# Batch 1's pairs 0 and 1 transposed by DMA instead of TensorE, with a third buffer for transposed keys and a new order of steps

## The chip, the cores and the metric

The kernel runs on one core of a Trainium2 chip. A core has five engines with an instruction queue each: TensorE (PE) multiplies matrices, VectorE (DVE), ScalarE (ACT) and GpSimd (POOL) work on elements, and SyncE (SP) only issues DMAs. GpSimd issues DMAs as well. The metric is the device time of one execution in microseconds (us); less is better.

## The reference

Attention with a sliding window of 96 keys and 8 global keys (4 batches, 8 heads, 768 tokens, head width 64), with a linear bias by distance, and behind it a SwiGLU block (512 to 1536 to 512) on all 3072 tokens. Inputs and outputs are 32-bit floats.

```python
scores = scale * np.matmul(q, k.transpose(0, 1, 3, 2))
rel = pos[:, None] - pos[None, :]
is_global = pos[None, :] < int(n_global)
is_local = (rel >= 0) & (rel < int(n_local))
dist = np.where(is_global & ~is_local, float(n_local), np.abs(rel).astype(np.float32))
scores = scores + (-slopes[:, None, None] * dist[None, :, :])[None, :, :, :]
scores = np.where(is_global | is_local, scores, -1000000000.0)
a = softmax(scores)            # with max subtracted
x = np.matmul(a, v), heads side by side: 3072 x 512
g = x @ w_gate
out = (g * sigmoid(g) * (x @ w_val)) @ w_out
```

## The kernel before

**Layout.** Scores are computed transposed: keys on the partitions, queries along the free dimension. So q and k must stand in SBUF with the head width on the partitions, which is a transpose of what lies in DRAM. Two heads make a pair (0 to 3) and fill 128 partitions together. Keys are cut into 7 chunks of 120, each with the 8 global keys in front (`kT`, a tile for each pair, used again by every batch). Values lie by the same chunks in `vS`, a buffer for a batch, three buffers in turn. Tokens of the SwiGLU block go in 8 stages of 384 (two for a batch).

**One list sets the order.** The whole program is a list of 1,092 named steps, the string `ORDER` (from line 37), read from left to right at the end of the kernel; the dictionary `WORK` maps a step's name to a function. A step `name.a.b` calls the function with these arguments. No scheduler moves anything: each engine executes its instructions in the order in which the list issues them, and waits at an instruction until its inputs and buffers are ready. The steps that matter here:

- Loads on GpSimd's queue (they convert from 32 to 16 bits on the way): `Lh` halves of heads of batch 0, `LG` all global values, `Lv.b.c` the values of batch b and chunk c (line 267), `L4.i.h` four heads of batch 1 at once (i is 0 for k, 1 for q), `Lr.b.i.h` the rows of one head (line 308), `Lw.w.n.g` parts of w_gate (w = 0) and w_val (w = 1) (line 315), `Lo.g` parts of w_out. `Lf`, `Li` and `Ld` are the first loads and the constants, on the queues of SyncE and ScalarE.
- Other work on GpSimd: `cast` where its last letter is P, `Z.b.P` (clears the tail of a value buffer) and `G.b.c0.c1.P` (copies global values into `vS`, line 282). A last letter V means VectorE, A ScalarE.
- `cast.i.p` converts first loads to 16 bits (line 352), `sl` and `M` make slopes and masks, `fill.n` runs n matmuls on constants.
- Batch 0 is transposed by TensorE: `T.p.half.i`, six transposes each, evacuated by `k` and `q`.
- Batch 1's pairs 0 and 1 are transposed by TensorE too: `U.p.i` (line 407, twelve transposes into one PSUM bank), evacuated by `kw.p` (keys) and `qw.p` (queries).
- All others go by DMA: `D.b.p.i` (line 435, on SyncE's queue) transposes pair p of the stage buffer. Queries go straight into `qT` (four buffers); keys go into `kN` (two buffers), from where `K.b.p` spreads them into the chunks of `kT` with three copies on VectorE (lines 442 to 446).
- Attention: `B` bias of batch 0 and `c.b.p.u` scores (TensorE, line 479), `x` exponentials (ScalarE), `m` masks (VectorE), `w.b.g.half.what` weighing (TensorE, line 540; what = 0 gives the sums, 1 and 2 the values), `n`, `i`, `r`, `p` divide by the sums and give `xT`.
- SwiGLU: `g.t.f` and `v.t.f` are the gate and value products of stage t and block f (four matmuls, line 590; `ga` and `gb` are halves of a `g`), `t` the tanh (ScalarE), `s` the sigmoid's product (VectorE, line 600), `h` the hidden row (VectorE), `o.t.i.part` the output product (three matmuls, line 631), `e` copies to SBUF and stores (SyncE's queue).

**Stage buffers.** A batch's k and q stand in `kst` and `qst` until they are transposed. These have two buffers each, dealt out in the order of the list: batch 0's first loads (32 bits) hold one and its other loads (16 bits) the second; batch 1 gets the first one again. Of batches 2 and 3, the one whose load comes first in the list gets the second one, and the other follows batch 1 in the first: its first load must wait until all K transposes of batch 1 have read there, and while it waits GpSimd's queue issues nothing behind it. Before, `Lr.2.0.0` is the earlier one and `Lr.3.0.1` the load that waits.

**The place of the change.** In the list before, the four `U` stand among the products of stage 1; `Lv.1.0` to `Lv.1.3` stand ahead of `Lr.3.0.1`, the load that waits for batch 1's stage buffer.

Of the kernel before, what the change touches and what calls it, by code (L numbers as in the profile page):

```python
# [42 lines left out]
c.0.3.0 x.0.2.0 T.1.1.0 Z.2.V Lh.1.1.4.8 T.1.1.1 c.0.2.1 x.0.3.0 G.0.1.4.V i.0.0.0 q.1.1.V T.0.1.1
B.3.1 c.0.3.1 T.0.1.0 Lv.0.3 k.1.1.A q.0.1.V k.0.1.V Lv.0.1 Lh.0.1.4.8 x.0.2.1 r.0.0.0 Lw.0.0.0
T.3.1.1 T.2.1.1 x.0.3.1 q.3.1.A c.0.1.3 c.0.0.2 w.0.1.0.0 i.0.1.0 Lw.0.0.1 q.2.1.A w.0.0.0.1
Lw.1.0.1 x.0.0.2 w.0.0.0.2 Lw.1.0.0 c.0.0.3 Lw.0.1.1 T.3.1.0 Lw.0.1.0 p.0.0.0.1.V r.0.1.0 T.2.1.0
Lw.1.1.0 x.0.1.3 x.0.0.3 Z.0.P p.0.0.0.0.V w.0.1.0.1 p.0.1.0.0.V w.0.1.0.2 p.0.1.0.1.V k.3.1.A
Lw.1.1.1 c.0.1.2 k.2.1.A ga.0.2 Lv.0.6 ga.0.0 ga.0.1 c.0.2.2 x.0.1.2 gb.0.0 m.0.0.2.V M.7.1 gb.0.1
# [12 lines left out]
x.1.1.1 h.1.1 o.0.0.0 v.1.11 g.1.9 v.1.9 s.1.5 v.1.5 g.1.7 t.1.7 g.1.3 t.1.9 Lr.1.1.6 m.1.0.1.V
D.1.2.1 m.1.0.0.V h.1.5 Lv.1.3 D.1.3.0 o.0.1.0 g.1.11 o.0.0.1 Lv.1.2 o.0.1.1 t.1.3 o.0.0.2 s.1.7
Lr.3.0.1 Lr.2.0.5 v.1.0 m.1.1.1.V o.0.1.2 o.0.1.3 D.1.3.1 t.1.11 s.1.9 s.1.3 s.1.11 o.0.0.3 h.1.0
v.1.3 h.1.11 m.1.1.0.V w.1.0.0.0 h.1.9 Lv.2.2 Lr.2.1.0 K.1.2 i.1.0.0 e.0.1 w.1.0.0.1 Lr.2.0.4 e.0.0
w.1.0.0.2 c.1.2.1 h.1.3 c.1.2.0 r.1.0.0 n.1.0.0 o.0.2.0 Lr.2.1.4 D.2.0.0 K.1.3 x.1.2.1 p.1.0.0.0.V
x.1.2.0 o.0.2.1 Lv.1.5 o.1.0.0 c.1.3.0 c.1.3.1 m.1.2.1.V c.1.0.2 o.0.2.2 o.1.0.1 x.1.3.0 m.1.3.0.V
# [38 lines left out]
o.4.1.1 s.5.8 o.4.1.2 h.5.6 v.5.8 x.3.0.2 o.4.1.3 t.5.9 p.3.1.0.0.V v.5.4 s.5.9 s.5.4 e.4.1 h.5.8
e.4.2 g.6.3 c.3.3.2 c.3.2.2 g.6.9 h.5.4 o.4.0.0 x.3.2.2 t.6.9 v.5.9 x.3.3.2 v.6.9 g.6.5 g.6.6 t.6.3
s.6.9 g.6.2 m.3.0.2.V h.6.9 g.6.1 t.6.6 t.6.5 s.6.6 g.6.4 o.4.0.1 o.4.0.2 v.6.5 s.6.3 m.3.3.2.V
s.6.5 t.6.1 v.6.4 t.6.2 h.5.9 v.6.1 g.6.8 o.4.0.3 s.6.1 h.6.5 s.6.2 m.3.2.2.V h.6.1 t.6.4 w.3.1.1.1
# [596 lines left out]
```

## Time and profile before

| | us |
|---|---|
| median of three runs | 240.96 |
| lowest and highest | 238.77, 241.08 |
| the profiled execution's own time | 239.84 |
| its span in the trace | 238.0 |

The span runs from the first to the last instruction that the profile has; some 1.8 us of the execution lie around it. The prediction shows lines of these views: the busy time of each engine (first the sum and the share of the span, then the number of instructions), strips of the span in 40 slices of 5.95 us with the busy share of each in tenths, the chain of waits that ended last, groups of instructions, and DMAs with their time from issue to landing. Rows of the chain and the timeline give the start, the length or busy time, the engine, the line of the code and the number of instructions; square brackets hold the idle time ahead of an instruction and what ended it. PE is TensorE, PEld its loading of weights, SPq the DMA queue of SyncE. The granted clock of TensorE was full in this execution (mean 1.0).

### The profile page before, as it was taken

What the parts mean: (1) busy time and instruction counts of PE and PEld (TensorE: products, weight loads), DVE (VectorE), ACT (ScalarE), POOL (GpSimd) and SP (SyncE); (2) the same over time, 40 slices, a digit from 0 to 9 for tenths busy, and PEclk for the clock granted to TensorE, in tenths of its full rate; (3) what the DMA queues carried; (4) which work ended last, traced back from release to release, by engine and by line L of the source; (5) the groups of instructions that cost most, each with busy time, mean ns of one, the idle gap of its engine ahead of it and who ended that gap; (6) DMA issues with size and microseconds to landing.
All of it is one profiled execution on the core that took longest, in us unless ns stands there. A gap on an engine that the chain in (4) does not pass through costs nothing.

```text
span 238.0 us, 5798 instructions
## 1 busy us (share of the span) xinstructions
PE 231.6 (97%) x2356; PEld 133.7 (56%) x2356; DVE 171.7 (72%) x411; ACT 117.5 (49%) x218; POOL 78.2 (33%) x99
## 2 busy tenths in 40 slices
PE   6999999999999999999999999999999999999994
PEld 4566566554556555555655654665555655555452
DVE  3799999767799976877948879889548854755400
ACT  3799813943776336377543366632453414223111
POOL 8874896720799845776000000000000000000000
PEclk9999999999999999999999999999999999999999
DMA  7999999999999999999974060100020101100114
GB/s 167 177 185 206 192 194 177 183 183 135 182 145 155 151 148 148 168 167 128 134 113 104 30 86 17 74 3 0 3 88 0 47 4 48 41 0 27 64 45 176
DMA packets 88715, 25.56 MB, mean 107 GB/s; under 512 B 78536, under 2 KB 85744, under 8 KB 88688
## 3 DMA queue, kind: packets, MB, share of 16 engines
q0 software_dynamic: 67520, 13.81, 70.9%
q1 hardware_dynamic: 20480, 10.80, 24.1%
q10 hardware_dynamic: 688, 0.59, 0.7%
q8 instruction: 18, 0.29, 0.6%
q14 instruction: 9, 0.07, 0.1%
HBM read 28.58 MB, written 6.29 MB: 146 GB/s over the span
## 4 chain that ended last, share of the span: by engine, by line
PE 89%; DMA 4%; ACT 3%; DVE 1%; issue 0%; SPq 0%; DVEq 0%; ACTq 0%
PE banks L590 52%; PE banks L631 25%; PE banks L540 5%; PE banks L479 4%; ACT at L489 2%; DMA dist<-dist_c 2%; DMA kN<-kst 2%; PE banks L620 1%; PE banks L466 1%; PE banks L369 1%; PE banks L407 1%; DVE xT L573 0%; DVE rb L563 0%; ACT masks L340 0%; ACT qT L398 0%
## 5 line engine op out<-in xcount | busy, mean ns | idle before, releaser
L596 ACT ACTIVATE th<-banks 128x384 f32<-128x384 f32 x96 | 44.7, 493 | 71.1 <-PE banks L590 68.0
L590 PE MATMUL banks<-xT,wv 128*128 128x384 f16 x384 | 72.7, 326 | 0.1
L590 PE MATMUL banks<-xT,wg 128*128 128x384 f16 x384 | 72.3, 326 | 0.1
L631 PE MATMUL banks<-wo,hT 128*128 128x512 f16 x276 | 68.0, 379 | 0.3 <-DVE sl L600 0.3
L606 DVE TENSOR_TENSOR hT<-banks,sl 128x384 f16<-128x384 f32 x96 | 51.5, 552 | 20.9 <-PE banks L590 19.5
L600 DVE SCALAR_TENSOR_TENSOR sl<-th,banks 128x384 f32<-128x384 f32 x96 | 50.3, 546 | 16.5 <-ACT th L596 15.7
L590 PEld LDWEIGHTS <-wv 128*128 128x128 f16 x384 | 37.1, 98 | 27.8 <-issue 0.7
L590 PEld LDWEIGHTS <-wg 128*128 128x128 f16 x384 | 36.8, 98 | 26.3 <-issue 0.3
L489 ACT ACTIVATE at<-banks 128x864 f16<-128x864 f32 (+2 forms) x52 | 42.1, 842 | 9.2 <-PE banks L479 8.6
L631 PEld LDWEIGHTS <-hT 128*128 128x128 f16 x276 | 26.1, 98 | 27.5 <-issue 1.5
L508 DVE TENSOR_TENSOR at<-at,masks 128x864 f16<-128x864 f16 (+3 forms) x60 | 25.5, 470 | 3.9 <-ACT at L489 3.7
L267 POOL DMA_DIRECT2D vS<-in_v_dram x28 | 25.4, 914 | 7.0 <-DMA vS<-in_v_dram 2.3
L649 ACT ACTIVATE osb<-banks 128x512 f32<-128x512 f32 x23 | 13.5, 598 | 25.0 <-PE banks L631 23.4
L308 POOL DMA_DIRECT2D kst<-in_k_dram x20 | 17.1, 855 | 16.7 <-PE banks L540 12.1
L308 POOL DMA_DIRECT2D qst<-in_q_dram x20 | 17.0, 858 | 3.6 <-DMA wo<-in_moe_w_out_dram 1.0
L479 PE MATMUL banks<-qT,kT 64*128 64x216 f16 (+5 forms) x240 | 14.4, 240 | 0.0
L573 DVE TENSOR_TENSOR xT<-ns,rb 128x384 f16<-128x384 f32 x24 | 12.6, 548 | 0.1
L479 PEld LDWEIGHTS <-kT 64*128 64x128 f16 x240 | 8.3, 94 | 7.4 <-issue 5.9
L540 PE MATMUL banks<-at,vS 128*32 128x216 f16 (+6 forms) x576 | 12.0, 225 | 0.4 <-issue 0.4
L549 ACT COPY ns<-banks 128x768 f32<-128x768 f32 x12 | 9.6, 799 | 4.8 <-PE banks L540 4.7
L540 PEld LDWEIGHTS <-vS 128*32 128x32 f16 x576 | 9.8, 95 | 2.6 <-issue 2.2
L556 DVE STREAM_TRANSPOSE dT<-banks 128x384 f32<-128x384 f32 x16 | 9.2, 575 | 1.4 <-PE banks L540 1.2
(59 smaller groups left out, 116.5 us busy)
## 6 DMA issues: line engine op xcount, KB each, us to landing
out_dram<-osb SPq DMA_DIRECT2D x23, 256.0 KB, 2.2
vS<-in_v_dram POOLq DMA_DIRECT2D x24, 120.0 KB, 7.6
qst<-in_q_dram POOLq DMA_DIRECT2D x20, 96.0 KB, 8.1
kst<-in_k_dram POOLq DMA_DIRECT2D x20, 96.0 KB, 7.4
wg<-in_moe_w_gate_dram POOLq DMA_DIRECT2D x6, 256.0 KB, 9.2
wv<-in_moe_w_val_dram POOLq DMA_DIRECT2D x6, 256.0 KB, 8.9
wo<-in_moe_w_out_dram POOLq DMA_DIRECT2D x3, 512.0 KB, 8.6
q<-in_q_dram POOLq DMA_DIRECT2D x3, 192.0 KB, 7.0
```

What stands on the lines that cost most here:

```text
L267: nc.gpsimd.dma_start(out=v_of(b)[NG:NG + n, c, :, :], in_=v[b, :, KC * c:KC * c + n, :].rearrange("h p d -> p h d"))
L308: nc.gpsimd.dma_start(out=rows_of(i, b, h // 2)[:, :, h % 2, :], in_=KQ[i][b, h].rearrange("(t p) d -> p t d", p=128))
L479: nc.tensor.matmul(sc[:, hi, col:col + n], lhsT=kTs[hp][r, 128 * c:128 * c + 128], rhs=qTs[b, hp][r, q0:q0 + n], start=fresh, stop=True, s ...
L489: nc.scalar.activation(out=at[:, :, 0:w], in_=scs.pop((b, hp, u))[:, :, 0:w], func=AF.Exp, scale=scale)
L508: ENG[e].tensor_mul(a2, a2, m[:, :, m0:m0 + n])
L540: nc.tensor.matmul(dst[r, o:o + n], lhsT=vSs[b][:, c, 4 * g + j, what - 1::2] if what else ones[:, 0:32], rhs=ats[b, hp, u][:, j % 2, col: ...
L590: nc.tensor.matmul(gv[t, f, which][:, 0:TB], lhsT=w[:, c, 128 * f:128 * f + 128], rhs=xTs[t][:, c, :], start=(c == 0), stop=(c == NC - 1))
L596: nc.scalar.activation(out=th, in_=gv[t, f, 0][:, 0:TB], func=AF.Tanh, scale=0.5)
L600: nc.vector.scalar_tensor_tensor(out=sl, in0=gv[t, f, "t"], scalar=1.0, in1=gv[t, f, 0][:, 0:TB], op0=AluOp.add, op1=AluOp.mult)
L606: nc.vector.tensor_mul(hTs[t][:, f, :], gv[t, f, 1][:, 0:TB], gv[t, f, "s"])
L631: nc.tensor.matmul(ops_t[t, i], lhsT=hTs[t][:, f, 128 * i:128 * i + 128], rhs=wo[:, f, :], start=(f == 0), stop=(f == NFF - 1))
L649: nc.scalar.mul(out=osb, in_=ops, mul=0.5)
```

## The change

- The steps `U`, `kw`, `qw` and `L4` leave the list; their functions stay in the code, unused.
- Batch 1's keys and queries of heads 0 to 3 are now loaded row by row (eight more `Lr.1`, so sixteen in all), and `D.1.0.0`, `D.1.0.1`, `D.1.1.0`, `D.1.1.1` transpose them by DMA, `K.1.0` and `K.1.1` spread the keys.
- `kN` has three buffers.
- The list is a new one from the first step on. In its head, the first loads and casts stand in another order and `cast.1.0` is on GpSimd instead of VectorE; `fill.14` and `fill.2` stand together; `G.0.4.7.P` stands among the weight loads instead of behind them. `Lr.3.0.4` stands ahead of all loads of batch 2, so that batch 3 gets the second `kst` buffer and batch 2 follows batch 1 in the first. `Lr.2.0.1`, the first load that needs batch 1's `kst` buffer again, stands ahead of `Lv.1.0` to `Lv.1.3`. Later parts are in another order too, with the same steps.
- The program has 2308 matmuls and transposes on TensorE in place of 2356, 24 DMA transposes in place of 20, and 98 loads on GpSimd's queue in place of 92.

The diff, cut to what is spoken of (a line of three dots stands for lines left out; the rest of the list holds the same steps as before in another order):

```diff
 ORDER = """
-Lf.A.1.1 Lf.S.0.1 LG pre cast.1.1.V fill.14 Li T.1.0.1 Lf.A.1.0 sl.3 cast.0.1.A sl.2 T.1.0.0 Ld.S
-B.1.0 Lf.S.0.0 B.1.1 k.1.0.V Lh.1.0.4.8 sl.1 cast.1.0.V fill.2 q.1.0.V cast.0.0.A sl.0 sl.6 sl.5
-T.0.0.1 c.0.1.1 T.0.0.0 c.0.1.0 M.3.1 T.3.0.1 T.2.0.1 q.0.0.A x.0.1.1 B.0.0 Lh.0.0.4.8 k.0.0.V B.0.1
...
-g.0.4 g.0.6 m.0.2.3.V Lw.1.2.0 g.0.5 h.0.1 v.0.6 G.0.4.7.P t.0.4 h.0.3 t.0.7 L4.0.0 M.3.0 s.0.4
-Lr.1.1.7 m.0.3.2.V v.0.5 v.0.7 r.0.0.1 v.0.4 g.0.9 t.0.6 t.0.5 s.0.7 s.0.5 s.0.6 L4.1.0 h.0.5 Z.3.P
-g.0.10 h.0.6 h.0.7 w.0.1.1.0 Lr.1.1.4 w.0.0.1.1 w.0.1.1.1 w.0.1.1.2 w.0.0.1.2 t.0.9 s.0.9 i.0.1.1
-Lr.1.0.6 p.0.0.1.0.V r.0.1.1 t.0.10 Lr.1.0.4 Lr.2.0.0 Lr.1.0.7 Lo.0 Lv.1.0 g.0.8 p.0.0.1.1.V
-Lr.2.0.1 g.0.11 v.0.10 p.0.1.1.1.V Lv.1.1 v.0.11 p.0.1.1.0.V t.0.11 g.1.8 s.0.11 h.0.11 t.0.8 g.1.1
-t.1.1 g.1.2 s.0.10 v.1.8 g.1.4 h.0.4 h.0.10 s.0.8 s.1.1 U.0.0 U.1.1 t.1.8 U.0.1 U.1.0 t.1.2 s.1.8
-Lo.1 qw.0.A s.1.2 Lr.1.0.5 Lr.1.1.5 g.1.6 M.4.0 h.1.8 v.0.9 kw.0.V qw.1.V M.6.0 M.7.0 v.1.2 g.1.0
-kw.1.A h.0.9 h.1.2 t.1.4 v.1.6 M.0.0 t.1.6 c.1.0.1 t.1.0 s.1.4 s.1.6 c.1.1.0 x.1.1.0 D.1.2.0 Z.1.V
...
+Lf.A.1.0 Lf.S.0.1 Li LG pre Lh.1.0.4.8 Lh.0.0.4.8 Lf.A.1.1 cast.1.1.V Ld.S Z.0.P cast.1.0.P sl.3
+fill.14 fill.2 sl.2 T.0.0.1 cast.0.1.A M.5.1 Lh.0.1.0.4 Lv.0.3 T.1.0.0 Lf.S.0.0 T.1.0.1 sl.0
+Lh.1.1.0.4 M.0.1 B.1.0 k.1.0.V cast.0.0.A sl.4 T.0.0.0 q.1.0.A B.1.1 M.3.1 c.0.1.1 q.0.0.A sl.1
...
+g.0.7 Lw.1.2.1 h.0.1 g.0.4 v.0.6 t.0.7 h.0.3 s.0.6 x.0.2.3 Lw.1.2.0 g.0.5 h.0.2 s.0.7 m.0.3.2.V
+v.0.5 t.0.4 Lo.0 m.0.3.3.V v.0.7 g.0.11 s.0.4 Lr.1.1.3 h.0.6 Lr.1.0.0 g.0.9 m.0.2.3.V w.0.1.1.0
+t.0.5 t.0.9 Lr.1.0.4 M.2.0 w.0.1.1.1 Lr.1.1.2 s.0.5 Lr.1.1.5 w.0.1.1.2 h.0.7 h.0.5 w.0.0.1.2
+Lr.1.0.6 w.0.0.1.1 g.0.8 i.0.1.1 Lr.1.0.5 v.0.10 p.0.0.1.0.V p.0.0.1.1.V t.0.11 v.0.4 t.0.8 s.0.11
+Lr.1.1.1 v.0.8 r.0.1.1 v.0.11 Lr.3.0.4 s.0.8 g.0.10 Lo.1 M.1.0 p.0.1.1.1.V t.0.10 Lr.1.0.3
+p.0.1.1.0.V g.1.8 s.0.9 M.0.0 v.1.8 t.1.8 g.1.3 h.0.8 h.0.4 Lr.1.1.4 t.1.3 s.1.8 g.1.9 Lr.1.1.0
+g.1.0 t.1.0 Lr.1.0.2 Z.1.V h.0.11 g.1.1 v.0.9 s.1.3 v.1.6 s.0.10 D.1.1.0 g.1.4 D.1.1.1 s.1.0 h.0.9
...
+g.1.7 D.1.2.0 s.1.1 v.1.9 g.1.6 h.1.1 Lr.1.0.1 Lo.2 h.1.4 g.1.11 t.1.7 h.1.9 g.1.2 s.1.7 o.0.0.0
...
+v.1.0 D.1.2.1 v.1.7 Lr.1.1.7 Lr.1.1.6 o.0.1.1 D.1.3.0 K.1.1 h.1.6 h.1.11 K.1.2 o.0.1.2 c.1.1.0
+D.1.0.0 c.1.1.1 Lr.2.0.1 Lv.1.2 M.7.0 h.1.0 Z.2.V Lv.1.0 o.0.1.3 Lv.1.1 K.1.3 x.1.1.0 x.1.1.1
+o.0.0.2 Lv.1.3 K.1.0 m.1.1.0.V o.0.0.3 c.1.2.0 Lr.2.1.0 D.1.3.1 D.1.0.1 e.0.1 Lr.2.0.4 c.1.2.1
...
+m.1.0.1.V o.1.0.2 w.1.0.0.0 Lr.3.1.4 Lr.2.0.5 w.1.1.0.2 r.1.1.0 w.1.1.0.1 w.1.0.0.1 w.1.0.0.2
...
@@ tr_dma
-            dst = kNs[b, hp] = sb2.tile([128, S], FP16, name="kN", tag="kN", bufs=2)
+            dst = kNs[b, hp] = sb2.tile([128, S], FP16, name="kN", tag="kN", bufs=3)
```

More of the change, by code (lines that the diff above doesn't have):

```diff
@@ L43 @@
[L43 to L48, printed above, removed]
@@ L61 @@
[L61 to L66, printed above, removed]
@@ L105 @@
[L105 to L108, printed above, removed]
-w.3.0.1.1 s.6.4 h.6.4 t.6.8 w.3.1.1.2 w.3.1.1.0 w.3.0.1.0 e.4.0 i.3.1.1 i.3.0.1 w.3.0.1.2 g.6.0
-n.3.1.1 v.6.0 v.5.2 v.6.6 r.3.1.1 t.6.0 n.3.0.1 g.6.10 r.3.0.1 h.5.2 p.3.0.1.1.V s.6.0 g.6.7 v.6.3
@@ new lines @@
+T.2.0.1 sl.5 k.0.0.V x.0.1.1 c.0.1.0 B.0.1 c.0.0.1 G.0.1.4.V T.3.0.1 T.3.0.0 T.2.0.0 x.0.1.0 B.0.0
+q.2.0.V c.0.0.0 T.1.1.0 k.2.0.V x.0.0.1 B.2.0 q.3.0.V sl.7 c.0.2.0 sl.6 M.2.1 x.0.0.0 k.3.0.A
+k.1.1.V w.0.0.0.0 B.2.1 c.0.2.1 B.3.1 c.0.3.1 Lh.1.1.4.8 T.1.1.1 Lv.0.2 x.0.2.1 B.3.0 c.0.3.0
+i.0.0.0 q.1.1.V T.3.1.1 Lv.0.0 T.0.1.0 x.0.3.1 Lv.0.1 c.0.1.3 x.0.2.0 x.0.3.0 T.0.1.1 T.2.1.1
+q.3.1.V q.0.1.A Lh.0.1.4.8 r.0.0.0 w.0.1.0.0 w.0.1.0.2 M.5.0 k.0.1.V Lw.0.0.0 Lw.0.0.1 i.0.1.0
+q.2.1.A w.0.0.0.1 p.0.0.0.0.V r.0.1.0 x.0.1.3 w.0.0.0.2 c.0.0.2 x.0.0.2 w.0.1.0.1 c.0.1.2 Lw.1.0.0
@@ new lines @@
+o.1.0.3 p.1.0.0.1.V D.2.0.0 p.1.0.0.0.V m.1.0.2.V Lr.2.1.3 m.1.2.2.V g.2.6 x.1.3.2 g.2.5 m.1.3.2.V
+D.2.0.1 g.2.2 w.1.1.1.0 m.1.1.2.V e.1.0 Lr.2.0.3 w.1.0.1.0 t.2.6 w.1.1.1.2 w.1.1.1.1 s.2.6 i.1.1.1
+Lr.2.0.6 v.2.2 t.2.2 g.2.11 n.1.1.1 D.2.2.1 t.2.11 s.2.2 D.2.1.1 g.2.9 D.2.2.0 t.2.5 Lr.2.0.2
+D.2.3.0 Lr.2.1.7 i.1.0.1 Lr.3.1.0 w.1.0.1.1 w.1.0.1.2 n.1.0.1 g.2.3 r.1.1.1 t.2.9 s.2.11 v.2.11
+p.1.1.1.1.V s.2.5 v.2.6 g.2.4 s.2.9 v.2.3 h.2.2 Lr.2.1.6 t.2.3 s.2.3 g.2.1 v.2.5 Lr.3.0.6 K.2.0
+h.2.6 h.2.11 g.2.8 Lv.2.1 g.2.7 Lv.2.3 t.2.1 s.2.1 v.2.4 D.2.1.0 h.2.3 t.2.4 D.2.3.1 o.1.2.0
@@ new lines @@
+g.4.7 t.4.3 t.4.10 h.4.6 w.2.1.1.1 D.3.3.1 s.4.10 e.3.1 w.2.1.1.2 h.4.0 w.2.1.1.0 s.4.3 t.4.7
+w.2.0.1.2 K.3.0 w.2.0.1.0 n.2.1.1 w.2.0.1.1 g.4.8 n.2.0.1 K.3.2 s.4.7 D.3.1.1 i.2.1.1 e.2.0 g.4.11
+t.4.11 t.4.8 K.3.1 v.4.3 Lv.3.1 o.3.2.0 c.3.0.1 i.2.0.1 h.4.3 c.3.1.1 v.4.7 o.3.2.1 s.4.8 o.3.2.2
+r.2.1.1 h.4.7 x.3.0.1 c.3.3.0 x.3.1.1 c.3.2.0 c.3.0.0 x.3.3.0 s.4.11 r.2.0.1 o.3.0.0 o.3.0.1
+p.2.1.1.0.V o.3.2.3 x.3.0.0 o.3.0.2 x.3.2.0 c.3.2.1 p.2.1.1.1.V c.3.3.1 c.3.1.0 m.3.0.1.V e.3.2
+x.3.1.0 m.3.1.1.V p.2.0.1.0.V p.2.0.1.1.V x.3.3.1 m.3.3.0.V o.3.0.3 g.5.5 o.4.2.0 m.3.1.0.V x.3.2.1
@@ L121 @@
+v.7.5 s.7.3 h.7.5 o.6.2.1 t.7.7 s.7.8 v.7.3 v.7.9 o.6.1.2 v.7.8 s.7.10 o.6.2.2 o.6.0.2 o.6.0.3 h.7.9
+s.7.7 h.7.3 e.6.0 v.7.7 o.7.1.0 g.7.6 h.7.8 t.7.6 v.7.6 o.6.2.3 h.7.7 o.7.0.0 v.7.10 s.7.6 h.7.6
+o.6.1.3 o.7.2.0 h.7.10 o.7.2.1 o.7.0.1 e.6.2 o.7.0.2 e.7.2 o.7.1.1 e.6.1 o.7.0.3 o.7.1.2 o.7.1.3
+o.7.2.2 e.7.0 e.7.1 o.7.2.3 e.7.3
 """
```

101 lines of the change are left out of this document (47 added, 54 removed).

## The prediction

> **What bounds the kernel now.** I read the shares of busy time first, then the strips, then the chain that ended last.
>
> ```profile
> PE 231.6 (97%) x2356; PEld 133.7 (56%) x2356; DVE 171.7 (72%) x411; ACT 117.5 (49%) x218; POOL 78.2 (33%) x99
> PE   6999999999999999999999999999999999999994
> DMA  7999999999999999999974060100020101100114
> PE 89%; DMA 4%; ACT 3%; DVE 1%; issue 0%; SPq 0%; DVEq 0%; ACTq 0%
> ```
>
> TensorE is busy in every slice but the first and the last, and holds 89% of the chain. The DMA engines are full for the first half (the strip stays at 9 up to slice 19, about 119 us) and then nearly idle. So TensorE's own work sets the end, and a load or a transpose counts only where TensorE reaches a step before its data. The chain in order of time gives the prices of TensorE's steps (start, length, instructions):
>
> ```profile
> 19.41 1.14 PE banks L590 x6
> 40.53 1.46 PE banks L407 x48
> 45.50 0.48 PE banks L479 x8
> 57.71 1.94 PE banks L631 x9
> 67.11 0.92 PE banks L540 x48
> 81.35 3.90 PE banks L590 x24
> ```
>
> A product step (four matmuls) is 3.90/6 = 0.65, an output step 1.94/3 = 0.65, a half step `ga` or `gb` 0.33, a score step 0.48/2 = 0.24, a weighing step 0.92/3 = 0.31. The first product starts at 19.41; from there TensorE's timeline shows only two waits worth naming:
>
> ```profile
> 123.09 0.42 PEld L590 LDWEIGHTS <-wv 128*128 128x128 f16 x3 [0.33 <-issue]
> 142.22 1.46 PE L631 MATMUL banks<-wo,hT 128*128 128x512 f16 x6 [0.32 <-DVE sl L600]
> ```
>
> So little is left to win by removing waits: 0.65. Whatever the change brings must come out of TensorE's work, and the question is which new wait it makes.
>
> **Part 1, the four `U` steps go.** The 48 transposes are the L407 row of the chain: -1.46, all of it on the path. Their evacuations (`kw`, `qw`) leave ACT and VectorE, which are not on the path there. Order details: `c.0.0.3` now stands behind the first product instead of ahead of it, +0.24 after 19.41. Of the two waits above, the second follows on a K transpose that had to wait for one of two `kN` buffers; the third buffer should free it, but a new order makes small waits of its own, so I count -0.3 (bounds 0 and -0.65).
>
> **Part 2, the head.** Its first part is rearranged. The rows that matter:
>
> ```profile
> 3.71 0.95 POOL L267 DMA_DIRECT2D vS<-in_v_dram x1
> 4.27 0.57 DVE L352 CAST q<-q 128x384 f16<-128x384 f32 x1 [2.47 <-DMA q<-in_q_dram]
> 7.20 0.51 ACT L352 CAST k<-k 128x384 f16<-128x384 f32 x1 [2.78 <-DMA k<-in_k_dram]
> 8.02 0.32 PE L479 MATMUL banks<-qT,kT 64*128 64x144 f16 x4
> 27.57 1.65 POOL L282 COPY vS<-vG 8x1536 f16<-8x1536 f16 x1
> ```
>
> `cast.1.0` moves from VectorE to GpSimd, and every later load of the POOL queue stands behind it. It cannot start before the first q load is in, 4.27. No row has a cast on GpSimd; the copy of 1536 elements a partition at 1.65 gives 0.41 for 384 by its length and 1.65 as the upper end; I take 0.6, since the instruction must have a fixed part. The fourth load is then issued at about 4.9 instead of 3.71. Cover: the three loads ahead of it are still under way (a load takes some 8 us from issue to landing, rows below), so the engines do not run dry. `G.0.4.7.P`, 1.65 on GpSimd, moves in among the weight loads under the same cover. If the cover fails, weights come 1.2 to 3.9 later. On TensorE `T.0.0.0` now stands ahead of `B.1.1` and `c.0.1.1`, and it needs the k load that lands at 7.20; the first scores come some 0.5 later than 8.02. ACT fills its 2.78 idle time with two masks in return. Sum of the head 0, bounds -0.5 and +0.8.
>
> **Part 3, the weights.** The same 25 loads stand ahead of `Lw.1.2.0` (the last of w_val) in both orders.
>
> ```profile
> 26.86 0.72 POOL L315 DMA_DIRECT2D wv<-in_moe_w_val_dram x1 [0.54 <-DMA wv<-in_moe_w_val_dram]
> 35.81 1.46 PE L590 MATMUL banks<-xT,wv 128*128 128x384 f16 x8
> ```
> ```profile
> DMA packets 12892, 3.99 MB, mean 186 GB/s; under 512 B 9952, under 2 KB 12889, under 8 KB 12889
> wo<-in_moe_w_out_dram POOLq DMA_DIRECT2D x3, 512.0 KB, 8.6
> kst<-in_k_dram POOLq DMA_DIRECT2D x6, 96.0 KB, 7.9
> kst<-in_k_dram POOLq DMA_DIRECT2D x1, 384.0 KB, 8.1
> vS<-in_v_dram POOLq DMA_DIRECT2D x3, 120.0 KB, 8.5
> wv<-in_moe_w_val_dram POOLq DMA_DIRECT2D x1, 256.0 KB, 8.5
> ```
>
> (The second fence is the view of DMA issues in the stretch 26.5 to 48: KB each, median us to landing.) It lands at 26.86 + 8.5 = 35.4. Its first user is `v.0.10`, at 35.81 before. In the new order 15 product steps, 6 half steps, 5 score and 6 weighing steps stand between the first product and `v.0.10`: 9.75 + 1.98 + 1.20 + 1.86 = 14.8, so 34.2, and some 0.6 more for the changes from one kind of step to another (35.81 against the same count before: 17 x 0.65 + 1.98 + 4 x 0.24 + 1.86 = 15.85, 35.26, difference 0.55). TensorE comes at 34.8 and waits 0.6 (bounds 0 and, with the cover of part 2 gone, 3.9).
>
> **Part 4, batch 1 by DMA.** Two loads of 384 KB become eight of 96 KB, the same bytes but eight issues of GpSimd instead of two, some 5 more of its time (0.84 each by the row at 61.23 below). After `Lw.1.2.0` and up to `Lr.1.0.2`, which the first transpose `D.1.1.0` needs, the new queue has two w_out loads and thirteen rows: 2 x 512 + 13 x 96 = 2272 KB, 2.33 MB at 186 GB/s = 12.5, so 47.9. The same count before (to `Lr.1.0.5`, 2800 KB) gives 50.8, and its transpose started at 51.12; I add that 0.3 and some issue time: `D.1.1.0` starts at 48.5. What transposes cost:
>
> ```profile
> 51.12 1.34 SPq L435 DMA_TRANSPOSE kN<-kst  x1
> 56.83 1.99 SPq L435 DMA_TRANSPOSE qT<-qst  x1
> ```
> ```profile
> kN<-kst SPq DMA_TRANSPOSE x1, 7.6
> ```
> ```profile
> kN<-kst SPq DMA_TRANSPOSE x3, 6.6
> qT<-qst SPq DMA_TRANSPOSE x2, 3.9
> ```
> ```profile
> kN<-kst SPq DMA_TRANSPOSE x2, 8.8
> qT<-qst SPq DMA_TRANSPOSE x2, 10.6
> ```
> ```profile
> kN<-kst SPq DMA_TRANSPOSE x4, 2.8
> ```
>
> These are the issues at 51.1, in 51 to 61, in 78 to 92 and in 113 to 140, in us to landing: 2.8 with an empty load queue, 7.6 behind a few loads, 8.8 to 10.6 while GpSimd keeps issuing. The four transposes of batch 1 before were all down by 56.83 + 3.9 = 60.7.
>
> Who waits for them? GpSimd's queue stands still until the K transposes of batch 1 have read their stage buffer:
>
> ```profile
> 47.29 1.86 POOL L267 DMA_DIRECT2D vS<-in_v_dram x2 [0.36 <-DMA vS<-in_v_dram]
> 61.23 1.68 POOL L308 DMA_DIRECT2D kst<-in_k_dram x2 [12.08 <-PE banks L540]
> 62.89 0.95 POOL L267 DMA_DIRECT2D vS<-in_v_dram x1
> ```
> ```profile
> vS<-in_v_dram POOLq DMA_DIRECT2D x3, 120.0 KB, 5.0
> ```
>
> The row names TensorE, which had long been done; 61.23 is half a us after the transposes landed. Before, `Lv.1.0` to `Lv.1.3` (values of batch 1) stood ahead of this halt; in the new order they stand behind `Lr.2.0.1`, which halts. So their landing hangs on the last K transpose, `D.1.0.0`. It is the fourth, takes the first `kN` buffer again, and so waits for `K.1.1`, which waits for `D.1.1.0`:
>
> ```profile
> 59.67 0.34 DVE L442 COPY kT<-kN 128x720 f16<-128x720 f16 x1
> 60.00 0.17 DVE L445 COPY kT<-kN 128x56 f16<-128x56 f16 x1
> ```
>
> `D.1.1.0` 48.5 + 7.6 = 56.1; `K.1.1` (three copies, 59.67 to 60.17) 0.5 and some 0.2 of hand-over, 56.8; `D.1.0.0` from 56.8 with 3.9, the row with GpSimd halted as here, 60.7; GpSimd goes on at 61.2. The fifth load from there is the last value load: 61.2 + 0.85 + 3 x 0.95 = 64.9, lands 5.0 later, 69.9 at most 70. TensorE wants it at `w.1.1.0.2`: 45 product, 17 output, 6 half, 15 score and 8 weighing steps, 29.25 + 11.05 + 1.98 + 3.6 + 2.48 = 48.4, so 67.8, and 1.2 for changes of kind (before, the same count for this step gives 65.8,
>
> ```profile
> 67.04 0.72 PE L540 MATMUL banks<-at,vS 128*32 128x216 f16 x32
> ```
>
> and it ran at 67.04). TensorE comes at 69.0 and waits 0.9. With `D.1.0.0` at 2.8 the wait is nothing, at 8.8 it is 5.8: bounds 0 and 5.8. The 0.6 of part 3 would move TensorE later and eat into it; I leave that margin for the scores `c.1.1.0`, which TensorE reaches at about 57.0 with `K.1.1` done at 56.8, an equal race. VectorE too stands in `K.1.3` and `K.1.0` with masks of batch 1 queued behind, which `w.1.1.0.0` needs; they hang on the same landing. The four extra loads behind the halt cost GpSimd some 4 more up to the end of its queue; the DMA strip has room from 119 on, batch 3 is transposed from 113 to 140: nothing.
>
> [...]
>
> **Sum.** 239.84 (the profiled execution; span 238.0) - 1.46 + 0.24 - 0.3 + 0 + 0.6 + 0.9 = 239.8. That execution is 1.12 under the median of three, 240.96, and inside their 238.77 to 241.08. On the median's scale the same sum is 240.9; I say 240.3, between the two.
>
> **Rivals.** (a) The transposes land as with an empty queue, 2.8, and the weights in time: no new wait, the old ones gone, 239.84 - 1.46 + 0.24 - 0.65 = 238.0, 239.1 on the median's scale. For it: 2.8 is the row whenever loads are done. Against: at 48.5 some 900 KB of loads are still queued, nearly 5 us. [...]
> (b) Slower: `D.1.0.0` lands late, because loads and five transposes share the engines as in 78 to 92. With 8.8 GpSimd goes on at 66.1, the values come 5.8 after TensorE wants them, 244.7; with 10.6 for `D.1.1.0` as well, 3.0 more, 247.7. From 64.7 on, 3.5 late, it decides for slower. For it: one step hangs on a chain of two transposes, a copy and five loads, with nothing to spare. Against: GpSimd issues nothing new in that time.
> (c) The cover in the head fails and the weights come late: 2.0 to 3.9 more, 241.8 to 243.7.
> That the change does not do what it says is excluded: the new program has 48 fewer matmuls and 24 transposes in place of 20.
>
> **Chances.** Forecast 0.32, (a) 0.20, (b) 0.34, (c) 0.14. About 1% is what a measurement of this kernel can tell from no change, 238.55 to 243.4 around the median. (a) ends below that in three of four cases, 0.15; (b) above it in 0.32; (c) in half. Faster 0.15, same 0.46, slower 0.39. The range reaches from (a) to the further half of (b): 237.9 to 246.5. The forecast's own range is 238.6 to 241.8.
>
> **What would show it.** L407 gone from the chain and no new TensorE wait over 1 us: the forecast or (a). TensorE idle before a L540 step near 69 with `vS` as its releaser, or before L479 near 57: part 4, and its length tells forecast from (b). GpSimd's longest halt should end near 61; at 65 or later it is (b). TensorE idle between 22 and 36 before L590 with `wg` or `wv` as releaser: part 3 or (c). The forecast is wrong if the first product starts a us off 19.4, or if batches 2 and 3 show waits that no part here has.

## The result and the profile after

| | kernel before | changed kernel |
|---|---|---|
| median of 20 runs, us | 240.09 | 241.51 |
| lowest, highest | 238.69, 241.12 | 239.94, 242.63 |
| ratio, 95% interval | | 1.0061, 1.0037 to 1.0085 |
| profiled execution: time, span | 239.84, 238.0 | 239.97, 238.2 |

The change costs 0.6%, 1.4 us between the medians. The forecast was 240.3, a small gain; the time lies inside its range, on the other side of no change. One caution for reading the traces: the changed kernel's profiled execution is among the fastest of its twenty, the other's is near its median. So the two traces show 0.2 of the 1.4, and the rest has to be read from other executions that begin with the same steps.

The page of the changed kernel: sums and shares, then strips of 5.95 us a slice, then the chain that ended last.

```profile
PE 230.6 (97%) x2308; PEld 131.9 (55%) x2308; DVE 169.7 (71%) x411; ACT 116.8 (49%) x214; POOL 83.1 (35%) x106
PE   7799999999999999999999999999999999999992
PEclk9799999999999999999999999999999999999999
PE 93%; DMA 2%; ACT 2%; SPq 1%; DVE 0%; issue 0%; DVEq 0%
```

48 instructions are gone from TensorE, but only 1.0 of its busy time, and two digits in the second slice are new: TensorE busy 7 where it was 9, its clock 7. In windows of 1 us (length, busy time and count of PE, PEld, DVE, ACT and POOL, then granted clock, DMA share, GB/s):

```profile
6.00:7.00 1.00, 0.78 (x8) 0.26 (x8) 1.00 (x8) 0.76 (x2) 1.00 (x2) 1.00 1.35 184
7.00:8.00 1.00, 0.00 (x0) 0.00 (x0) 0.44 (x2) 0.78 (x3) 1.00 (x2) 1.00 1.47 164
8.00:9.00 1.00, 0.96 (x20) 0.78 (x20) 0.56 (x2) 1.00 (x3) 1.00 (x2) 0.91 1.59 187
9.00:10.00 1.00, 1.00 (x14) 0.48 (x10) 1.00 (x4) 0.74 (x3) 1.00 (x3) 0.50 1.91 170
...
12.00:13.00 1.00, 1.00 (x12) 0.42 (x12) 1.00 (x6) 0.31 (x1) 1.00 (x2) 0.88 2.01 166
```

The kernel before, for comparison: its clock strip, and TensorE's rows at the same place. The last row is `T.0.0.0`, which has two warm matmuls (`fill.2`), `T.0.0.1` and the first scores ahead of it and does not wait.

```profile
PEclk9999999999999999999999999999999999999999
```
```profile
7.04 0.59 PE L348 MATMUL banks<-ones 128*128 128x256 f16 x2
7.56 0.53 PE L369 MATMUL banks<-ident,q 128*64 128x128 f16 x6
8.28 0.53 PE L369 MATMUL banks<-ident,k 128*64 128x128 f16 x6
```

In the changed kernel TensorE stands still from 6.78 to 8.04, and soon after, the granted clock is one half for some 3.4 us (0.18 of the window at 8, where 0.91 was granted, three whole windows, 0.24 of the one at 12). The timeline of that place, the first product, and the rows of part 4, all of the changed kernel:

```profile
7.47 0.51 ACT L353 CAST k<-k 128x384 f16<-128x384 f32 x1 [0.22 <-DMA k<-in_k_dram]
8.04 0.36 PE L370 MATMUL banks<-ident,k 128*64 128x128 f16 x6 [1.25 <-ACT k L353]
20.56 0.48 PE L591 MATMUL banks<-xT,wg 128*128 128x384 f16 x2
57.59 0.54 PE L480 MATMUL banks<-qT,kT 64*128 64x216 f16 x8
60.51 0.82 POOL L309 DMA_DIRECT2D kst<-in_k_dram  x1 [12.52 <-DMA kN<-kst]
61.32 3.65 POOL L268 DMA_DIRECT2D vS<-in_v_dram  x4
70.24 1.25 PE L541 MATMUL banks<-at,vS 128*32 128x216 f16 x64
```

`T.0.0.0` needs the k load `Lf.S.0.0`, which lands at 7.45, and since the change nothing stands ahead of it to do meanwhile. The first product comes at 20.56 in place of 19.41. Behind that TensorE waits nowhere: the value loads are issued by 64.97 (61.32 + 3.65) and land just before 70.24.

The end, after and before:

```profile
233.14 0.83 PE L621 MATMUL banks<-wo,hT 128*128 128x128 f16 x12
234.44 0.39 SPq L646 DMA_DIRECT2D out_dram<-osb  x1
```
```profile
233.69 0.83 PE L620 MATMUL banks<-wo,hT 128*128 128x128 f16 x12
234.96 0.40 SPq L645 DMA_DIRECT2D out_dram<-osb  x1
```

TensorE ends at 233.97, 0.55 sooner. The account nearly fits: +1.15 at the first product, -1.46 for the transposes, +0.24 for `c.0.0.3`, and -0.65 for the two old waits make -0.72. But from the end of the last store's issue to the end of the span it takes 3.4 us (238.2 - 234.83) in place of 2.6 (238.0 - 235.36), which eats that up.

### The profile page after: what moved, and what is told of

Read it like the earlier page. It is cut to its first block, busy times and chain, and to the rows that moved or that the text cites. A ratio compares the mean times of both kernels' runs of the same rounds, so it can differ in the third digit from the quotient of the medians.

```text
span 238.2 us, 5717 instructions
## 1 busy us (share of the span) xinstructions
PE 230.6 (97%) x2308; PEld 131.9 (55%) x2308; DVE 169.7 (71%) x411; ACT 116.8 (49%) x214; POOL 83.1 (35%) x106
## 4 chain that ended last, share of the span: by engine, by line
PE 93%; DMA 2%; ACT 2%; SPq 1%; DVE 0%; issue 0%; DVEq 0%
PE banks L591 53%; PE banks L632 26%; PE banks L541 6%; PE banks L480 5%; DMA k<-in_k_dram 2%; PE banks L370 1%; PE banks L621 1%; PE banks L467 1%; ACT at L490 1%; ACT qT L399 0%; DVE kT L383 0%; ACT k L353 0%; SPq L260 0%; SPq L254 0%; SPq L257 0%
## 5 line engine op out<-in xcount | busy, mean ns | idle before, releaser
L591 PE MATMUL banks<-xT,wv 128*128 128x384 f16 x384 | 73.2, 326 | 0.0
L591 PE MATMUL banks<-xT,wg 128*128 128x384 f16 x384 | 71.3, 326 | 0.1
L632 PE MATMUL banks<-wo,hT 128*128 128x512 f16 x276 | 68.7, 379 | 0.0
L607 DVE TENSOR_TENSOR hT<-banks,sl 128x384 f16<-128x384 f32 x96 | 50.8, 549 | 20.5 <-PE banks L591 20.0
L601 DVE SCALAR_TENSOR_TENSOR sl<-th,banks 128x384 f32<-128x384 f32 x96 | 51.4, 548 | 19.2 <-ACT th L597 18.5
L591 PEld LDWEIGHTS <-wg 128*128 128x128 f16 x384 | 37.2, 98 | 26.4 <-issue 0.2
L591 PEld LDWEIGHTS <-wv 128*128 128x128 f16 x384 | 36.6, 98 | 26.9 <-issue 0.7
L490 ACT ACTIVATE at<-banks 128x864 f16<-128x864 f32 (+2 forms) x52 | 41.2, 835 | 15.9 <-PE banks L480 15.8
L309 POOL DMA_DIRECT2D kst<-in_k_dram x24 | 20.1, 845 | 16.0 <-DMA kN<-kst 12.5
L309 POOL DMA_DIRECT2D qst<-in_q_dram x24 | 20.1, 844 | 4.7 <-DMA kst<-in_k_dram 1.8
L550 ACT COPY ns<-banks 128x768 f32<-128x768 f32 x11 | 8.6, 805 | 7.5 <-PE banks L541 7.5
L574 DVE TENSOR_TENSOR xT<-ns,rb 128x384 f16<-128x384 f32 x22 | 11.4, 547 | 0.2
```

What stands on the lines that cost most here:

```text
L309: nc.gpsimd.dma_start(out=rows_of(i, b, h // 2)[:, :, h % 2, :], in_=KQ[i][b, h].rearrange("(t p) d -> p t d", p=128))
L490: nc.scalar.activation(out=at[:, :, 0:w], in_=scs.pop((b, hp, u))[:, :, 0:w], func=AF.Exp, scale=scale)
L591: nc.tensor.matmul(gv[t, f, which][:, 0:TB], lhsT=w[:, c, 128 * f:128 * f + 128], rhs=xTs[t][:, c, :], start=(c == 0), stop=(c == NC - 1))
L601: nc.vector.scalar_tensor_tensor(out=sl, in0=gv[t, f, "t"], scalar=1.0, in1=gv[t, f, 0][:, 0:TB], op0=AluOp.add, op1=AluOp.mult)
L607: nc.vector.tensor_mul(hTs[t][:, f, :], gv[t, f, 1][:, 0:TB], gv[t, f, "s"])
L632: nc.tensor.matmul(ops_t[t, i], lhsT=hTs[t][:, f, 128 * i:128 * i + 128], rhs=wo[:, f, :], start=(f == 0), stop=(f == NFF - 1))
```

## The experiments

All times are compared with the kernel before on the same chip in the same rounds, as a ratio with its 95% interval in brackets. Theory H: the loss is the head. Theories V and V2: it is the landing of batch 1's values and transposes. "Ones" in a name means that batch 1's weighing reads a constant tile, so that nothing waits for its values. "First product" is the start of the first L590 or L591 instruction of the profiled execution.

**Filling the gap, and the values ahead of the halt.**

```diff
 a1_fill_gap (the changed kernel; a3_both has both edits)
+fill.5
 T.0.0.0
 a2_values_first (the changed kernel)
-Lr.2.0.1
 Lv.1.2
...
 Lv.1.3
+Lr.2.0.1
```

> The changed kernel with five more warm matmuls ahead of T.0.0.0, where TensorE stands still from 6.78 to 8.04 us; nothing else. Theory H (the loss is that gap and the half clock behind it, 0.50 granted from about 8.9 to 12.1): the clock stays at 1.0, the first product starts at 19.1 to 19.5 instead of 20.56, and the time falls by 1.0 to 1.5 from the changed kernel's, less up to 0.9 that TensorE then waits at w.1.1.0.2 for values that land at 69.8: 0.3 faster to 0.5 us slower than the kernel before. Theory V (the loss is the late landing of batch 1's values and transposes): the clock may stay up, but the time stays 1 to 1.5 us above the kernel before.

> The changed kernel with Lr.2.0.1 moved behind Lv.1.3, so that the four value loads of batch 1 no longer stand behind the halt. Theory H: the dip of the clock in the first 13 us is still there, and the time is that of the changed kernel, 1.0 to 1.6 us above the kernel before; the values land before 62. Theory V: the time falls by 1 to 1.5 us, to that of the kernel before.

> Both edits. Theory H: no dip of the clock, no wait at w.1.1.0.2; 0.5 to 1.2 us faster than the kernel before, and by 0.3 to 0.9 faster than with the warm matmuls alone. Theory V: the same as with the value loads moved alone. If neither holds, it stays 1 us or more above the kernel before.

Measured, in this order: 1.0079 (1.0046 to 1.0111), 1.0283 (1.0233 to 1.0332) and 1.0239 (1.0194 to 1.0283). In the profiled execution of a1 the k load landed at 8.69, the five matmuls were over at 7.80, TensorE still waited 1.48, the clock was half for twice as long (10.6 to 17.4), and the first product came at 22.94. So the edit did not close the gap. In three of its eight runs the mean granted clock was 0.997 or more all the same, and these took 241.75 to 241.76, hardly less than the median of the eight, 241.80. The edit of a2 costs 5.3 us more than the changed kernel (1.0283 - 1.0061, of 240), and most of the reason is in its rows: TensorE's waits (a third one is 1.18 long, at 89.14), and DMA issues from 48 to 62 with their median time to landing.

```profile
60.95 0.55 PE L480 MATMUL banks<-qT,kT 64*128 64x216 f16 x8 [2.22 <-DMA qT<-qst]
65.02 0.55 PE L480 MATMUL banks<-qT,kT 64*128 64x216 f16 x8 [1.47 <-DMA qT<-qst]
```
```profile
vS<-in_v_dram POOLq DMA_DIRECT2D x4, 120.0 KB, 12.0
kN<-kst SPq DMA_TRANSPOSE x4, 7.6
qT<-qst SPq DMA_TRANSPOSE x2, 10.2
```

The same view of the changed kernel:

```profile
kN<-kst SPq DMA_TRANSPOSE x4, 3.7
qT<-qst SPq DMA_TRANSPOSE x4, 4.4
```

With four value loads beside them the transposes take about twice as long to land. So GpSimd's halt of 12.5 us is no loss here: while it lasts, no new load stands beside the transposes.

**The warm matmuls alone.**

```diff
 b1_before_fill_moved (the kernel before)
 fill.14
+fill.2
...
-fill.2
 q.1.0.V
```

> The kernel before with its fill.2 moved up behind fill.14, as the changed kernel has it; nothing else. Theory H: TensorE stands still from about 7.2 to 7.6 or longer ahead of T.0.0.1, and if the share of idle time is what lowers the clock, the granted clock falls to half for some 3 us and the time rises by 0.8 to 1.6 us. If a gap of this length does not lower the clock, the time changes by less than 0.3. Theory V: no change, within 0.3.

Measured: 0.9990 (0.9956 to 1.0024). The gap opened (0.43 and 0.90) and in the profiled execution the clock was half from 9.1 to 12.5, but in 8 of 12 runs the mean granted clock was 0.997 or more. The four others took 240.24 to 241.24, these eight 238.52 to 239.67: the lowered clock goes with the longer times. But in the kernel before, the place of the two warm matmuls alone costs nothing that can be measured over all twelve.

**Values that nobody waits for, first try; the old head; TensorE's transposes back.**

```diff
 x1_other_values
-lhsT=vSs[b][:, c, 4 * g + j, what - 1::2]
+lhsT=vSs[0 if b == 1 else b][:, c, 4 * g + j, what - 1::2]
 h1_old_head
+the first 75 steps of the kernel before (Z.2.V left where the change has it), then the changed list without them
 u1_tensor_transposes_back
-Lr.1.0.0 Lr.1.0.1 Lr.1.0.2 Lr.1.0.3 Lr.1.1.0 Lr.1.1.1 Lr.1.1.2 Lr.1.1.3
-D.1.0.0 D.1.0.1 D.1.1.0 D.1.1.1 K.1.0 K.1.1
+L4.0.0 L4.1.0 U.1.0 kw.1.V U.1.1 qw.1.A U.0.0 kw.0.V U.0.1 qw.0.A
```

> The changed kernel, in which batch 1's weighing reads batch 0's values; batch 1's own values are loaded as before and not read, so batch 1's output is another. Theory V2 (the loss is the landing of batch 1's values behind GpSimd's halt: they land at 70 to 72, TensorE wants them at 68.8 when the head runs at full clock, and a dip of the clock in the head only uses up time that it would have waited): the time falls by 1.2 to 2.2 us from the changed kernel's, to between 0.8 faster and 0.4 slower than the kernel before. Theory H (the dip in the head alone): no change, 1.0 to 2.2 us above the kernel before.

> The changed kernel with the first 75 steps (loads, casts, transposes and scores of the first 15 us) in the order of the kernel before, and the rest in the changed order. Theory V2: the clock stays up in most runs, the first product starts at 19.0 to 19.8, and TensorE waits 1 to 3 us at a weighing step near 69 with vS as releaser; the time stays 1.0 to 2.2 us above the kernel before. Theory H: no such wait, the time falls to 0.5 to 1.3 us below the kernel before.

> The changed kernel with batch 1's pairs 0 and 1 transposed by TensorE again, and two loads of 384 KB in place of eight of 96 KB; all else in the changed order. Theory V2: the last K transpose of batch 1 is now D.1.3.0, GpSimd goes on 2 to 5 us sooner, the values land before TensorE wants them, and the time is that of the changed kernel plus 1.46 less the wait of 1 to 2.5: 0 to 1.5 us above the kernel before. Theory H: the changed kernel plus 1.46, 2.5 to 3.5 us above the kernel before.

x1 gave 1.0817 (the same edit on h1, run h2, 1.0814). The edit makes a wait of its own: batch 0's value buffer is the one that batch 2 takes next, and in the trace of x1 VectorE's clearing of a value buffer (line 286) waits 17.48 for a value load, up to 76.92, and TensorE then 13.43 for the keys that VectorE spreads behind it. How the edit ties these together stays open. The run says nothing of either theory. h1 gave 1.0024 (0.9998 to 1.0050): the clock was 0.997 or more in 11 of 12 runs, but the two lists did not fit together: four waits of 0.3 to 0.7 between 8 and 20.8 put the first product at 21.39, and TensorE waited 0.37 for `vS` at 71.87. u1 gave 1.0139 (1.0106 to 1.0172), above the changed kernel's interval: with this head, the DMA transposes are worth some 1.9 us (1.0139 - 1.0061, of 240).

**A mended head order, ones in place of values, transposes sooner.**

```diff
 a4_head_order (the changed kernel)
-M.0.1 B.1.0 k.1.0.V cast.0.0.A sl.4 T.0.0.0 q.1.0.A B.1.1 M.3.1 c.0.1.1 q.0.0.A sl.1
-T.2.0.1 sl.5 k.0.0.V x.0.1.1 c.0.1.0 B.0.1 c.0.0.1
+q.1.0.A M.0.1 B.1.0 k.1.0.V cast.0.0.A sl.4 B.1.1 M.3.1 c.0.1.1 q.0.0.A sl.1
+sl.5 x.0.1.1 c.0.1.0 B.0.1 T.0.0.0 k.0.0.V T.2.0.1 c.0.0.1
 x3_ones (the changed order)
-lhsT=vSs[b][:, c, 4 * g + j, what - 1::2] if what else ones[:, 0:32],
+lhsT=vSs[b][:, c, 4 * g + j, what - 1::2] if what and b != 1 else ones[:, 0:32],
 v6_transposes_sooner (on a4)
-D.1.2.1
...
 D.1.0.0
+D.1.2.1
...
-c.1.2.0 c.1.2.1
 o.1.1.0 g.1.10
+c.1.2.0 c.1.2.1
```

> The changed kernel with four steps of its head moved: q.1.0.A ahead of the masks M.0.1 and the cast that waits for the last k load, and B.1.1, c.0.1.1, c.0.1.0 and B.0.1 ahead of T.0.0.0. Theory H (TensorE's wait ahead of T.0.0.0, 1.25 to 2.7 us by the load, and the half clock behind it are the loss): the wait falls under 0.8, the clock stays at 1.0 in most runs, the first product starts at 19.0 to 19.8, and the time falls by 1.5 to 2.5 us from the changed kernel's, below the kernel before by 0.3 or more. Theory V2 (the values of batch 1 land at 70 to 72 and set the time): the first product is as early, but TensorE then waits 1 to 3 us for vS near 69, and the time stays 0.3 to 2 us above the kernel before.

> The changed kernel, its own head, with batch 1's weighing reading the tile of ones. Theory H: the time of the changed kernel, 1.0 to 1.6 us above the kernel before, since the head alone costs that. Theory V2: 1 us or more below the changed kernel. If both head and values bind at nearly the same time, as the traces of the runs so far have it (TensorE there at 70.2 to 72.6, values landed 69.8 to 71.9), it gains 0 to 0.5.

> The kernel with the mended head, and D.1.2.1 moved behind D.1.0.0 on SyncE's queue, with c.1.2.0 and c.1.2.1 behind o.1.1.0 and g.1.10 on TensorE. Theory V2: the halt of GpSimd ends about 1.2 us sooner, the values land 1 us sooner, and the time is about 1 us under that of the mended head alone. Theory H: no gain over the mended head alone. If the scores c.1.2.0 wait instead, 0 to 1.5 us are lost there.

a4: 1.0096 (1.0064 to 1.0129), a miss: `B.0.1` now waited 1.59 for a bank that the exponential `x.0.1.1` frees, and the clock fell all the same (with ones 1.0093, no better). x3: 1.0052 (1.0024 to 1.0080) against the changed kernel's 1.0061. Its first product came at 21.40 behind a wait of 2.17 ahead of `T.0.0.0` (the k load landed at 8.32), with no wait of TensorE over 0.15 behind it. With this head the values' landing is worth nothing that can be measured. v6: 1.0134 (1.0079 to 1.0189); GpSimd went on 0.6 sooner than in a4 (60.98 against 61.61), the values landed at 71.06 in place of 71.15, and TensorE waited 0.65 at `c.1.3.*`.

**The head by itself, and the changed order with a clean head.**

```diff
 ah_new_head_in_before
+the first 64 steps of the changed kernel, then the list of before without them
 h3_old_first_steps
+the first 32 steps of the kernel before, M.5.1 M.0.1 ahead of cast.0.0.A, then the changed list without them
 h3_ones: the same with ones in place of batch 1's values
 f12_warm (the changed kernel)
+fill.12 (ahead of T.0.0.0)
```

> The kernel before with the first 64 steps of the changed kernel (up to about 13 us) and the rest in its own order; batch 1 is transposed by TensorE as before. Theory H: TensorE waits 1.2 to 2.7 us ahead of T.0.0.0, the clock falls to half for 3 or 6 us, the first product starts at 20.5 to 22.5, and the time rises by 1.2 to 2.5 us over the kernel before. If the head is not the loss, within 0.5 us of the kernel before.

> The changed kernel with the first 32 steps of the kernel before (M.5.1 and M.0.1 kept ahead of cast.0.0.A). Theory H: no wait over 0.8 ahead of T.0.0.0, clock 1.0 in most runs, first product at 19.0 to 19.9, time 0.5 to 1.5 us below the kernel before. Theory V2: the first product as early, but TensorE waits 1 to 2.5 us for vS at a weighing step near 69, and the time is 0 to 1 us above the kernel before.

> The same with batch 1's weighing reading the tile of ones in place of the values (batch 1's output is another). Theory V2: 1 us or more faster than with the values, 0.8 to 1.6 below the kernel before. Theory H: within 0.4 us of the run with the values.

> The changed kernel with twelve warm matmuls (0.2 us each) ahead of T.0.0.0, enough to cover its wait up to about 9.2. Theory H (the half clock in the head is the loss): the clock stays at 1.0 in most runs, the first product starts at 20.0 to 20.7 in place of 20.6 to 22.9 in the runs so far, and the time falls by 1.0 to 1.8 us from the changed kernel's, to that of the kernel before within 0.5. Theory V2 (the values' landing at 70 to 72 sets the time): less than 0.6 us is gained, and TensorE waits for vS near 70.

ah: 1.0139 (1.0098 to 1.0180), 242.83 against 239.88. With this head the kernel before loses 2.95 us. Some of it belongs to the joining of the two lists: behind the head TensorE has waits of 0.51 at 19.66 and 0.72 at 30.10 that neither kernel has. Its timeline shows the rest:

```profile
8.34 0.36 PE L369 MATMUL banks<-ident,k 128*64 128x128 f16 x6 [1.38 <-ACT k L352]
21.71 1.14 PE L590 MATMUL banks<-xT,wg 128*128 128x384 f16 x6
```

h3: 1.0041 (1.0011 to 1.0072), with the clock at 0.996 or more in all 12 runs and the first product at 19.38. The head is mended, and it is still not faster than before. The chain that ended last tells why (shares of the span by engine; then rows from it, with start, length, what):

```profile
PE 68%; DMA 20%; POOL 7%; issue 2%; DVE 1%; POOLq 0%; DVEq 0%
```
```profile
18.65 7.38 DMA wg<-in_moe_w_gate_dram
...
27.57 10.50 DMA wo<-in_moe_w_out_dram
...
43.21 6.26 DMA kst<-in_k_dram
...
49.49 8.10 DMA kN<-kst
...
59.10 2.82 DMA kN<-kst
...
63.39 2.73 POOL vS L267 x3
66.13 5.90 DMA vS<-in_v_dram
72.03 0.04 issue
72.08 1.01 PE banks L540 x50
```

TensorE is not in it before 72. It runs from load to load, through `D.1.1.0` (8.10 to landing) and `D.1.0.0`, through the end of GpSimd's halt to the last values, which land at 72.03. In the changed kernel TensorE held 93% of this view. TensorE's rows at batch 1's first scores, h3 and then h3_ones:

```profile
58.24 0.25 PE L479 MATMUL banks<-qT,kT 64*128 64x216 f16 x1 [1.05 <-DMA qT<-qst]
58.64 0.83 PE L479 MATMUL banks<-qT,kT 64*128 64x216 f16 x7 [0.15 <-DVE hT L606]
```
```profile
58.40 0.55 PE L479 MATMUL banks<-qT,kT 64*128 64x216 f16 x8 [1.76 <-DMA qT<-qst]
```

What the head no longer loses, TensorE loses behind it, most of all to `D.1.1.1`, the queries, ahead of `c.1.1.0`. From the first product to TensorE's last matmul it takes 216.2 us in h3 (235.61 - 19.38), 213.4 in the changed kernel (233.97 - 20.56), with the same steps between, and 215.1 in the kernel before (234.52 - 19.41). Counting the same matmul of both traces from the first product, h3 falls 0.7 behind up to `v.0.10`, where TensorE's weight loads wait for `wv` and `wg` (0.39 at 23.19, 0.33 at 26.07, 0.62 at 35.57; the changed kernel has no such row), 1.8 more at `c.1.1.0`, and 0.3 more at batch 1's values, at 72.08: together the 2.8. At `c.1.1.0` of h3 the keys were spread at 58.13 and the queries landed at 58.20, nearly together; in h3_ones the queries' transpose, landed at 58.36, was the later one by 1.7.

h3_ones: 1.0023 (0.9991 to 1.0054), 0.2% under h3 with overlapping intervals. f12: 1.0089 (1.0054 to 1.0123), a miss: the twelve matmuls took 1.3 us, not 2.4, ended at 8.04, and the load landed at 8.61. The mean clock was 1.0 in two of its runs, at 241.40 and 242.33 us: a full clock alone does not bring the time back.

**The scores later.**

```diff
 k3_scores_later (on h3), k3_scores_later_ones (on h3_ones)
 o.0.1.2
-c.1.1.0 c.1.1.1
...
 o.0.1.3
-x.1.1.0 x.1.1.1
 o.0.0.2
-m.1.1.0.V
 o.0.0.3
+c.1.1.0 c.1.1.1 x.1.1.0 x.1.1.1 m.1.1.0.V
 c.1.2.0
```

> The kernel with the first 32 steps of the old head and ones in place of batch 1's values, and c.1.1.0, c.1.1.1 with what follows on them moved behind o.0.1.3, o.0.0.2 and o.0.0.3, 1.95 us later on TensorE (batch 1's output is another). Theory K (batch 1's first scores wait for the transposes, and that wait gives back the saving): no wait over 0.5 us between 56 and 64, and 0.8 to 1.8 us faster than the same kernel with the scores in their old place, 0.6 to 1.6 us below the kernel before. If the wait only moves to c.1.2.0 or c.1.3.0 behind it, less than 0.5 us is gained.

> The same with the values read. Theory K alone: as fast as with ones, 0.6 to 1.6 us below the kernel before. Theory K with the values next: TensorE comes to the weighing steps near 70.0 and waits 1 to 2 us for vS, and the time is that of the run with the old first steps, 0 to 1 us above the kernel before.

1.0045 (1.0013 to 1.0077) and 1.0065 (1.0037 to 1.0092). The wait for the queries is gone in both traces, and the edit has made a wait of its own: with four score steps in a row TensorE waits for banks (rows of k3_scores_later).

```profile
59.71 0.36 PE L479 MATMUL banks<-qT,kT 64*128 64x216 f16 x4 [0.80 <-ACT at L489]
60.49 0.36 PE L479 MATMUL banks<-qT,kT 64*128 64x216 f16 x4 [0.42 <-ACT at L489]
```

So theory K, that the wait at `c.1.1.0` is all that gives the saving back, was neither shown nor refuted; the 0.7 at the weights speaks against "all". No version with the DMA transposes beats the kernel before.

## Why the prediction was wrong, step by step

- **Part 1, -1.46 - 0.3 + 0.24.** Right: L407 is gone, and in the profiled execution both old waits too. From the first product to the last matmul it is 1.7 less (213.4 against 215.1; forecast 1.5). The DMA transposes are worth 0.8% as long as the head is late (u1 against the changed kernel).
- **Part 2, "Sum of the head 0, bounds -0.5 and +0.8".** This is the step that failed. I had seen that `T.0.0.0` now stands ahead of `B.1.1` and `c.0.1.1`, and counted 0.5 later for the first scores; they came at 8.60, 0.6 later. I did not ask how long TensorE stands still meanwhile and what its clock is behind that, although the load's landing was in my rows. The first product came 1.15 later in the profiled execution, past the 1 us that the prediction had named as a sign of being wrong, and at 21.40, 21.63 and 22.21 in x3, a2 and u1, which begin with the same steps (the k load, at 7.45 there, landed at 8.32 in x3 and 7.54 in a2). So a term put at 0, at most 0.8, was 1.15 to 2.8. The head in the kernel before (ah) makes 1.39%, two waits of the joining included.
- **Part 2, the load and the clock.** From the landing of the k load to the first product it took 13.07 to 13.15 us in the changed kernel, x3, f12 and a3, where the half clock lasted 3.4, and 14.09 and 14.25 in a2 and a1, where it lasted 6.8 (13.67 in x1, where the 6.8 began before the load had landed). So with this head the lateness of that load passes on in full, and by these rows a second stretch of half clock behind it costs about 1.0. In the kernel before it took 12.23 (19.41 - 7.18). The mean granted clock is below 0.997 in 19 of the changed kernel's 20 runs, and 0.997 or more in 88 of the 103 runs of the kernel before that stood beside the experiments. In the changed kernel's trace the clock fell after a gap of 1.25, with TensorE busy for 4.75 of the 6 us around it (6 to 12). But the length of the gap does not decide by itself: gaps of 1.24 in k3_scores_later_ones and 1.35 in h2, also ahead of 9 us, left the clock at 1.0, and no run here shows what makes the difference.
- **Part 3, +0.6 at the weights.** 0 in the changed kernel, whose TensorE came late. In h3, where it came to `v.0.10` at 35.34 (forecast 34.8), 0.24 shows as idle there and 0.7 was lost up to it: with a clean head this part was nearly right.
- **Part 4, +0.9 at the values.** The chain was read rightly: the halt ended at 60.51 (forecast 61.2), the last value load was issued by 64.97 (64.9) and landed by 70 (70). The wait was 0 because TensorE was not there at 69.0 but at 70.24. What I called an equal race at `c.1.1.0` I left without a price, and I watched the keys there; the queries' transpose behind them on SyncE's queue landed with them in h3 and 1.7 later in h3_ones. With a clean head the wait there is 1.05 to 1.76 in its row, and the values land at 72, not 70.
- **The rivals.** (a) needed the transposes at 2.8; they took 6.3 in the changed kernel (`D.1.1.0`, issued at 48.14) and 8.1 in h3. (b), that the transposes and the values set the time, comes nearest to h3, but not as it was told: `D.1.0.0` landed in 2.8 there, `D.1.1.0` was the slow one, and TensorE lost 1.8 at the queries and 0.3 at the values, not 5.8. In the changed kernel it did not happen. Neither did (c): `cast.1.0` took 0.50 on GpSimd (forecast 0.6), and the weights were in time. The slower side had a mechanism that no rival of mine named.
- **The number.** That the time lies inside the range is luck: +1.5 of waits that did not come stood in for the head's loss. The gain in the forecast did not come from the sum, which gave 239.82 for 239.84, but from a middle value between the scale of one execution and that of a median of three, 240.96; over twenty runs the kernel before has 240.09.

So two losses hide each other. Either the head is late and the weights and transposes are in time (1.0061), or the head is clean and TensorE waits for them (1.0041). That is why mending one gained next to nothing. The head's 2.95 and the transposes' -1.9 add up to 1.05, near the 1.4 measured and within the intervals, but the second holds only behind a late head.

Open: how much of the head's loss is the standing still and how much the first stretch of half clock (the runs meant to part them kept the gap, none of their profiled executions kept the clock, and the runs of a1 and f12 with a full clock were no faster); why the span ends later behind the last store; whether the third `kN` buffer does anything by itself, which wasn't tried; and whether a list with a clean head and scores that wait for neither queries nor banks would gain.

## What to carry to other kernels

Where a step is moved ahead of others on TensorE, look at what it waits for and what is left to fill that time: early in this program a microsecond of standing still was often followed by several at half clock (1.25 by 3.4 in the changed kernel and 1.48 by 6.8 in a1, but 1.24 by none in k3_scores_later_ones). Replacing TensorE's work by DMA helped here only as far as the DMA chain had slack (worth some 1.9 us behind the late head, by u1; with the clean head of h3 TensorE lost 1.8 at the queries); price each landing against TensorE's arrival, queries as well as keys, before counting the removed instructions as saved. And where a late engine hides another wait, test the parts in both orders, since undoing one alone can seem to do nothing; TensorE's time from one fixed step to its last matmul tells the two apart.
